# A fused retention and phase-mixing kernel: the first third of its written order laid out anew

## The chip, the cores and the metric

The kernel runs on one core of a Trainium2 chip, as one program. The metric is device time in microseconds, the median of several executions. The core has a matrix engine (TensorE, PE in the profile; its weight loads are listed apart as PEld), a vector engine (DVE), an activation engine (ACT), a general engine (POOL) and a queue engine for transfers (SP). Each runs its own list of instructions in order, and an instruction that depends on another engine's waits for its semaphore. ACT, POOL and SP also issue DMA transfers.

## The reference

Inputs are q, k, v of shape (4, 8, 768, 64) and four weights, all float32.

```python
gamma = 1.0 - 2.0 ** (-5.0 - np.arange(H))
for t in range(S):
    state = gamma * state + outer(k[:, :, t], v[:, :, t])
    y[:, :, t] = q[:, :, t] @ state / np.sqrt(D)
x = y.transpose(0, 2, 1, 3).reshape(B, S, H * D)
theta = x @ w_theta
yr = einsum('ts,bsd->btd', w_tok_r, x * cos(theta))
yi = einsum('ts,bsd->btd', w_tok_i, x * sin(theta))
u = x + yr + yi
out = u + maximum(u @ w_ch, 0)
```

A recurrence with a decay per head comes first, then a mixing over tokens with phases, then a layer over channels. The output is (4, 768, 512), float32.

## The kernel before, in words

The recurrence is computed in chunks: 24 units, each 256 tokens of one batch for four of the eight heads (unit n: batch n // 6, chunk n % 6 // 2, half of the heads n % 2). The mixing works on 24 tiles C of 128 tokens by 512 channels, six to a batch; the units 2i and 2i + 1 make the tiles 2i and 2i + 1.

Nothing is scheduled by a program: the string `ORDER` (lines 22 to 86) names 929 steps, and the loop at line 616 records them one after another. Each engine executes its share of them in that order. A step is `name.numbers.engine`; the last letter says who does it: p POOL, v DVE, a ACT, s SP (for loads and stores a and s are the queue that issues the transfer). The steps that matter here:

- Lk, Lq, Lv (lines 163 to 170, issue at 157): load k, q, v of a unit, 256 KB each. The built program gives the transfers of SP and ACT eight semaphores in turn, so each one waits until the one eight before it has landed, whichever of the two queues it is on.
- Pth, Pw.r.g, Pch (173, 182, 176): theta's weight (wth), the token weights in three row groups each (r = 0 real, 1 imaginary; g of 1, 2 and 3 blocks of 128 rows, 192, 384 and 576 KB in bfloat16), the channel weight (wch). POOL issues them, and they become bfloat16 on the way.
- const8, const9 (line 233): the decay factors qx, eight exponentials on ACT, const8 for the first 256 tokens, const9 for the rest. const7 brings in the sine table.
- ck, cq, cqs, cv (137/139, 302, 308): cast or scale k, q, v to bfloat16 (kqb, vb).
- Tk, Tq (316) transpose k and q on PE into one bank kq_ps; E copies it out as kqT.
- A (346): scores; m (355): their mask, on DVE, into at; Y (423): scores times v; I (411): state times q; ST (373): the unit's new state. S0, S1 (391, 395) carry the state on, SB copies it as bfloat16 for I.
- XB, XA (139/137, 441): the unit's result becomes xT, half of a tile. Tx (455) transposes the tile back, Ex copies it as x_sb.
- Hh.C (469): theta, four matmuls into a bank of the tag acc; CN.C.w (476): its cosine and sine, on ACT, into cs (two buffers); z.C (483): x times both.
- Tw.r.t (491) transposes a block of rows of a token weight, Ew copies it to wtr or wti.
- M.t.s (509): the two matmuls of the token mixing for output tile t and source tile s; M.t.* needs Tw and Ew of row block t % 6. u, Tu or Du, Eu, O, f, SO: the sum with x, its transpose, the channel layer, the result, its store.
- Z (278): filler, two matmuls of zeros each.

PSUM has two banks for the tag acc (Z, Hh, M, O) and two for tr (kq_ps, x_ps, w_ps, u_ps); a step that writes a bank waits until the last reader of what stood there is done. So Hh.C waits until CN has read the theta that had the bank, and Tk, Tx, Tw wait for E, Ex, Ew.

```python
def load_unit(name, src, n, e):
    t = io.tile([P, HU, 2, D], FT, ..., bufs=9 if name == "vf" else 16)
    queues[e].dma_start(out=..., in_=...)

def CN(C, w):
    st["cs", C] = work.tile([P, 2, dm], BF, name="cs", bufs=2)
    nc.scalar.activation(st["cs", C][:, w, :], st["th_ps", C], AF.Sin, ...)
```

Of the kernel before, what the change touches and what calls it, by code (L numbers as in the profile page):

```python
# [45 lines left out]
Lv.11.s XB.9.1.a XB.9.0.a f.2 M.4.0 O.1 M.4.1 cqs.14.p m.10 S0.10.v f.1 cq.11.a ck.12.v M.4.4 M.4.2
Tu.3 Eu.3.a Dx.9 SB.10.0.a cqs.12.p u.4 Hh.9 Tq.11 ck.11.v Tu.4 z.6.v Eu.4.v ck.15.v M.5.0 M.5.4
Tk.11 E.11.a SB.10.1.p cv.11.p M.5.2 M.5.3 I.10 M.5.5 M.5.1 Lq.13.a A.11 Y.10 ck.14.v ST.11 CN.9.1
CN.9.0 SO.0.a Hh.8 u.5 S0.11.v z.9.v XB.10.0.v m.11 Dk.12 Tx.8 Tq.14 O.4 Lv.13.a SB.11.0.a Lq.15.s
Lk.13.s CN.8.1 Lk.18.a XB.10.1.a CN.8.0 SB.11.1.p cv.12.p Lq.16.s I.11 Tk.14 Ex.8.v A.12 Y.11 ST.12  # L50
f.4 Lv.15.s O.3 z.8.p E.14.a XA.11.0 XA.11.1 Hh.10 S0.12.a f.3 SB.12.0.v Tx.10 Tu.5 CN.10.1 Dx.11
Ex.10.v cq.13.p Lk.16.s Lv.17.s Hh.11 SO.2.s CN.10.0 m.12 S1.12 z.10.v Tk.15 M.6.1 M.6.2 M.6.0 M.6.3
CN.11.0 CN.11.1 M.7.3 SB.12.1.a Lk.17.a ck.13.a M.7.4 M.7.0 M.6.4 Dk.13 M.7.1 z.11.v M.6.5 SO.3.s
A.14 M.7.2 Eu.5.v I.12 Lv.14.s u.6 cqs.15.v M.7.5 M.9.3 Tq.15 ck.17.a E.15.a m.14 SO.4.a Lq.17.s
Lq.18.s Lk.21.s ck.16.a M.9.0 M.9.5 M.9.1 M.9.4 Lq.19.a M.9.2 Du.6 cv.13.v u.7 M.8.0 u.9 Y.12
cv.14.p ST.13 A.13 O.5 XB.12.1.a XB.12.0.a M.8.1 S0.13.a S1.13 M.8.4 M.8.3 SB.13.0.a SB.13.1.p
cq.16.p m.13 I.13 ck.18.a Y.13 ST.14 A.15 f.5 cq.17.v Lv.18.a M.8.5 M.8.2 XA.13.0 XA.13.1 S0.14.v
SB.14.0.p Lv.16.s Hh.13 S1.14 u.8 Tx.12 M.10.1 cv.15.p cv.17.p SB.14.1.p M.10.0 M.10.4 cqs.18.v
M.10.5 CN.13.0 CN.13.1 Hh.12 CN.12.1 I.14 m.15 Y.14 CN.12.0 ST.15 S0.15.v XB.14.1.a SB.15.0.a M.10.3
cv.16.v Dk.16 Dk.17 Du.7 Dx.13 M.10.2 Dk.18 O.6 SB.15.1.p XB.14.0.v S1.15 I.15 Y.15 ST.16 SO.5.a  # L60
cv.18.p f.6 S0.16.v A.16 M.11.4 SB.16.1.p M.11.1 Lq.21.a Ex.12.a z.12.p SB.16.0.a Lk.19.s Lk.20.s
XB.15.0.a u.10 z.13.p XB.15.1.a m.16 O.7 Du.10 I.16 Y.16 ST.17 f.7 A.17 Tu.8 Hh.15 CN.15.1 CN.15.0
# [9 lines left out]
cv.21.v u.14 A.21 ST.21 CN.19.0 CN.19.1 S0.21.v M.15.3 M.15.5 S1.21 m.21 XA.20.1 Hh.18 CN.18.1  # L72
CN.18.0 Dx.18 Dk.22 ck.23.a M.15.4 M.15.2 SB.21.0.p M.15.1 M.15.0 SB.21.1.v Lv.23.s Du.12 Dx.19
XA.20.0 O.9 f.9 I.21 Y.21 A.22 ST.22 M.16.1 cqs.23.p u.15 m.22 S0.22.v z.18.p z.19.p M.16.5
SB.22.0.p M.16.4 O.12 M.16.0 SO.8.a M.16.2 M.16.3 SB.22.1.p XB.21.0.a XB.21.1.a SO.11.s Du.14
cv.23.p Dk.23 f.12 Du.13 Dx.20 Dx.21 Hh.21 u.16 I.22 A.23 Y.22 ST.23 CN.21.0 CN.21.1 Hh.20 CN.20.1
# [570 lines left out]
```

## Time and profile before

| | |
|---|---|
| time, median of 3 runs | 165.22 us (165.19 to 165.68) |
| span of the profiled execution, from its first to its last instruction | 163.6 us |
| TensorE busy | 155.2 us, 95% |
| DVE, ACT, POOL busy | 114.0, 78.9, 74.3 us |
| moved by DMA | 34.93 MB, 214 GB/s over the span |

The profile is of one execution of its own, and its span leaves out what lies ahead of the first and behind the last instruction; the times of the runs include that. The difference to the median is 1.6 us. Lines such as L476 are lines of the kernel; copies made through the helper `copy` all stand at L137 (ACT) or L139 (DVE and POOL), so the tile names tell them apart. In a group, "out<-in" are tiles. The time in brackets is how long the engine stood idle just before, and whose work ended that.

### The profile page before, as it was taken

To read this page: it belongs to the slowest core of one execution; us is meant where nothing else is said; L and a number is where in the kernel's file an instruction comes from. 1 tells how busy PE (TensorE), PEld (TensorE's weight loads), DVE (VectorE), ACT (ScalarE), POOL (GpSimd) and SP (SyncE) were. 2 spreads that over 40 slices of the span, in tenths; PEclk is the share of its full clock that TensorE was granted. 3 is DMA by queue.
4 is the path that set the end of the run, shared out by engine and by line. 5 is a ranking of instruction groups with operands and counts; after the bars stand their busy time and mean duration, and the time that the engine had idled before them with its cause. 6 is when DMAs were issued, how large, how long until landed. Compare 5 with 4: busy or idle time off the path is not lost.

```text
span 163.6 us, 4928 instructions
## 1 busy us (share of the span) xinstructions
PE 155.2 (95%) x2034; PEld 87.2 (53%) x2034; DVE 114.0 (70%) x215; ACT 78.9 (48%) x140; POOL 74.3 (45%) x107
## 2 busy tenths in 40 slices
...
GB/s 115 297 290 255 268 283 236 275 220 286 220 162 232 223 291 139 338 203 270 324 263 198 134 268 221 242 193 298 125 245 136 103 92 227 160 64 128 129 164 224
DMA packets 69062, 34.93 MB, mean 214 GB/s; under 512 B 26416, under 2 KB 66096, under 8 KB 69040
## 3 DMA queue, kind: packets, MB, share of 16 engines
...
q0 software_dynamic: 2688, 3.41, 12.1%
...
q14 instruction: 6, 0.05, 0.1%
...
## 4 chain that ended last, share of the span: by engine, by line
PE 76%; DMA 8%; ACT 5%; POOL 3%; issue 2%; SPq 2%; DVE 1%; POOLq 0%; ACTq 0%
PE y_ps L509 36%; PE o_ps L536 11%; PE th_ps L469 10%; DMA kqf<-in_k_dram 8%; PE r_ps L423 3%; ACT qx L233 3%; PE w_ps L491 3%; PE at_ps L346 3%; PE r_ps L411 2%; PE kq_ps L316 2%; SPq L157 2%; PE y_ps L561 2%; ACT cs L476 1%; PE x_ps L455 1%; PE r_ps L373 1%
## 5 line engine op out<-in xcount | busy, mean ns | idle before, releaser
L509 PE MATMUL y_ps<-z,wtr 128*128 128x512 bf16 x138 | 52.4, 380 | 0.0
L509 PE MATMUL y_ps<-z,wti 128*128 128x512 bf16 x138 | 52.3, 379 | 0.0
L483 POOL TENSOR_TENSOR z<-cs,x_sb 128x1024 bf16<-128x1024 bf16 x12 | 25.5, 2136 | 17.9 <-ACT cs L476 10.0
L355 DVE TENSOR_TENSOR at<-at_ps,mask 128x1024 bf16<-128x1024 f32 x24 | 29.2, 1216 | 0.2
L469 PE MATMUL th_ps<-wth,xT 128*128 128x512 bf16 x96 | 24.5, 379 | 0.5 <-ACT cs L476 0.4
L516 DVE TENSOR_TENSOR u<-y_ps,x_sb 128x512 bf16<-128x512 f32 x23 | 15.8, 688 | 12.7 <-PE y_ps L509 12.6
L542 DVE SCALAR_TENSOR_TENSOR ot<-o_ps,u 128x512 f32<-128x512 f32 x22 | 15.1, 688 | 12.5 <-PE o_ps L536 12.4
L308 POOL TENSOR_TENSOR vb<-vf,vsc 128x512 bf16<-128x512 f32 x15 | 15.6, 1041 | 17.3 <-DMA vf<-in_v_dram 16.9
L476 ACT ACTIVATE cs<-th_ps,zerob 128x512 bf16<-128x512 f32 x24 | 16.4, 685 | 13.3 <-PE th_ps L469 8.8
L536 PE MATMUL o_ps<-wch,uT 128*128 128x512 bf16 x88 | 22.6, 379 | 0.0
L476 ACT ACTIVATE cs<-th_ps,halfpi 128x512 bf16<-128x512 f32 x24 | 16.3, 686 | 11.5 <-issue 5.4
L509 PEld LDWEIGHTS <-wtr 128*128 128x128 bf16 x138 | 13.5, 98 | 12.7
L509 PEld LDWEIGHTS <-wti 128*128 128x128 bf16 x138 | 13.5, 98 | 12.0 <-issue 0.2
L139 POOL CAST sbd<-s 64x256 bf16<-64x256 f32 (+1 forms) x21 | 10.1, 481 | 20.8 <-DVE s L391 17.7
L137 ACT COPY kqT<-kq_ps 128x1024 bf16<-128x1024 bf16 x12 | 12.1, 1012 | 11.9 <-PE kq_ps L316 11.9
L469 PEld LDWEIGHTS <-xT 128*128 128x128 bf16 x96 | 8.8, 98 | 8.7 <-issue 0.5
L137 ACT CAST kqb<-kqf 128x512 bf16<-128x512 f32 x16 | 9.6, 620 | 6.9 <-DMA kqf<-in_k_dram 6.3
L536 PEld LDWEIGHTS <-uT 128*128 128x128 bf16 x88 | 8.1, 98 | 8.3
L278 PE MATMUL zz<-zero 128*128 128x512 bf16 x30 | 10.3, 476 | 1.9 <-DVE zero L192 1.9
L423 PE MATMUL r_ps<-at,vb 64*64 64x128 bf16 x384 | 9.9, 221 | 1.6 <-DVE at L355 1.6
L316 PE MATMUL kq_ps<-ident,kqb 128*128 128x128 bf16 x120 | 11.2, 220 | 0.3 <-POOL kqb L302 0.3
L139 POOL CAST kqb<-kqf 128x512 bf16<-128x512 f32 x12 | 7.2, 612 | 8.5 <-DMA kqf<-in_k_dram 8.4
...
## 6 DMA issues: line engine op xcount, KB each, us to landing
...
```

The source lines that it names most:

```text
L137: nc.scalar.copy(dst, src)
L139: engines[e].tensor_copy(dst, src)
L308: engines[e].tensor_mul(in_blocks(vb), by_token(raw["vf", n]), _bcast_last(K["vsc"][:, i, :, h * HU:(h + 1) * HU], D))
L355: nc.vector.tensor_mul(at.rearrange("p g j a t -> p (g j) (a t)"), st["at_ps", n].rearrange("p g j a t -> p (g j) (a t)"), _bcast_mid(K["m ...
L423: nc.tensor.matmul(st["R", n + 1][c][g * D:(g + 1) * D, j * P:(j + 1) * P], st["vb", n][rows, lo:lo + D], st["at", n][rows, g, j, a, :], s ...
L469: nc.tensor.matmul(th_ps, st["xT", C][:, j, :], K["wth"][:, j, :], start=(j == 0), stop=(j == 3))
L476: nc.scalar.activation(st["cs", C][:, w, :], st["th_ps", C], AF.Sin, bias=K["zerob" if w else "halfpi"], scale=1.0)
L483: engines[e].tensor_mul(st["z", b][:, c], st["cs", C], _bcast_mid(x_of(C), 2))
L509: nc.tensor.matmul(st["y", t], K["wT"][r][:, s0, t0 * P:(t0 + 1) * P], st["z", b][:, s0, r, :], start=(done == 0 and r == 0), stop=(done = ...
L516: nc.vector.tensor_add(st["u", t], st["y", t], st["x", b][:, t0, :])
L536: nc.tensor.matmul(o_ps, st["uT", t][:, j, :], K["wch"][:, j, :], start=(j == 0), stop=(j == nD - 1))
L542: nc.vector.scalar_tensor_tensor(st["ot", t], st["o", t], 0.0, st["u", t], ALU.max, ALU.add)
```

## The change

`ORDER` is rewritten from its start up to the step M.3.4 (328 of its 929 steps); from M.3.4 on it is unchanged. The steps are the same ones. 47 of them are done by another engine, 12 loads are issued on the other queue, and most stand at another place. Nothing else in the code differs, except that the string is two lines shorter, so every line number behind it is lower by 2.

What moves, by kind:

- Casts and scalings: ck.2, ck.5 from ACT to POOL, cqs.2 from DVE to POOL, cqs.1 and cv.2 from POOL to DVE, cv.3 from DVE to POOL, ck.4 and cq.4 from POOL to ACT, cq.5 from ACT to DVE, and some of units 7 to 10.
- State copies: most SB up to unit 8 change engine; S0.1 goes from DVE to ACT.
- E.3 and E.6 go from ACT to DVE, Ew.1.0 and Ew.0.1 from DVE to ACT, z.2 from DVE to POOL.
- Exponentials: const8 stands behind ck.1 and the loads Lk.4 and Lq.4 instead of ahead of them.
- Theta: Pth stands behind cv.1 on POOL (ck.0, SB.0.1, cv.1, Pth), no longer behind cv.2 as well. On ACT CN.0 comes ahead of XB.3 and CN.1.0, and ck.6 and cq.6 stand on both sides of CN.1.1 instead of ck.6, cq.6 ahead of both halves of CN.1; CN.4 comes after Ew.1.0.
- Weight rows: Pw.0.1 and Pw.1.1 stand around z.0; Pw.1.2 moves behind z.2, cq.8, z.4 and ck.7, with Pch and Pw.0.2 behind it.
- Loads: Lq.1 and Lk.1 go out on ACT ahead of the exponentials; Lk.6 moves ahead of Lq.6, which goes to ACT's queue with Lv.6, Lv.7 and Lk.8; Lk.9 and Lv.8 move ahead on SP.

```diff
 ORDER = """
-const2 Lv.0.s const1 const6.v Z.29 Z.2 const5 Z.38 Lk.0.a const3 Z.35 Z.8 Lq.0.s Lv.1.s Z.28 constA
-const4 Lq.1.a const9 Lk.1.s Z.39 const8 ck.0.p Tk.0 ck.1.a cqs.0.v cv.0.v Tq.0 E.0.v Lq.4.a ST.0
-Lk.4.a cqs.1.p Tq.1 Lq.2.s S0.0.v SB.0.1.v A.0 Lk.2.s SB.0.0.p cv.1.p Lv.2.s S1.0 Z.15 I.0 Z.27 m.0
-Tk.1 E.1.a cqs.2.v Z.34 cv.2.p Y.0 ST.1 XB.0.1.a S0.1.v S1.1 SB.1.0.a Pth Lq.3.s Z.18 XB.0.0.v Tq.2
-A.1 SB.1.1.a ck.2.a I.1 m.1 Y.1 ST.2 Tk.2 const7 Z.23 XB.1.0.v Lk.3.s E.2.v XB.1.1.v A.2 ck.3.p
-S0.2.v m.2 S1.2 SB.2.1.a Z.11 cqs.3.p Tq.3 Lv.3.s Tx.0 Tk.3 Z.3 ck.4.p Lv.4.s Lk.5.s Lq.5.s Lv.5.s
-Lq.6.s Lk.6.s Lv.6.s Lq.7.s E.3.a SB.2.0.v I.2 Y.2 XB.2.1.a Ex.0.a cv.3.v cq.4.p Tk.4 Lq.8.s A.3
-ST.3 Lk.7.s S0.3.v SB.3.0.a S1.3 Lv.7.s Lk.8.s Tx.1 Tq.4 SB.3.1.p cv.4.p m.3 Pw.1.0 XB.2.0.a Ex.1.a
-I.3 Lv.8.s E.4.a ck.5.a cq.5.a Y.3 Pw.0.0 ST.4 Hh.0 S0.4.v XB.3.0.v XB.3.1.v cv.5.v CN.0.1 A.4
-CN.0.0 Tq.5 Hh.1 Tk.5 SB.4.0.p SB.4.1.a Pw.0.1 Hh.2 m.4 E.5.v I.4 Y.4 ST.5 ck.6.a Tk.6 Tx.2 cq.6.a
-CN.1.1 CN.1.0 XA.4.1 A.5 XA.4.0 m.5 Lq.9.s Ex.2.v S0.5.v z.0.p Tq.6 E.6.a CN.2.0 cv.6.p Hh.3
-SB.5.0.v Tx.3 Tw.1.0 z.1.v SB.5.1.a Ew.1.0.v Ex.3.a CN.2.1 A.6 I.5 Y.5 ST.6 XA.5.0 z.2.v Tw.0.0
-CN.3.0 Tx.4 CN.3.1 Ew.0.0.v S0.6.v XA.5.1 Ex.4.v Hh.4 CN.4.0 CN.4.1 Tw.0.1 M.0.1 Pw.1.1 z.3.v M.0.0
-Tw.0.2 Pw.1.2 Ew.0.2.a SB.6.1.a Hh.5 z.4.p SB.6.0.p Lk.9.a M.0.3 ck.7.p cqs.7.p M.0.2 CN.5.1 CN.5.0
-cq.8.v m.6 Ew.0.1.v Tw.1.1 Tw.1.2 Ew.1.1.v Lv.9.s M.0.4 M.1.0 Tx.5 Ew.1.2.v M.1.1 S1.6 Tk.7 M.1.4
-Pch Ex.5.v z.5.v cv.7.v Tq.8 Tq.7 M.1.2 E.7.a M.0.5 I.6 Y.6 ST.7 A.7 ck.8.a u.0 S0.7.v m.7 XA.6.1
-SB.7.1.a M.1.5 M.1.3 XA.6.0 Tw.1.3 M.2.5 Pw.0.2 M.2.3 u.1 S1.7 Tk.8 M.2.1 M.2.0 SB.7.0.v Ew.1.3.a
-Tu.0 I.7 cv.8.v E.8.a Lk.10.s ck.10.p cv.9.p Y.7 ST.8 A.8 cqs.9.v ck.9.v M.2.4 Du.1 Eu.0.a XB.7.1.a
-XB.7.0.v S0.8.v SB.8.0.v M.2.2 Tx.6 Tq.9 Tk.9 Lv.10.a cv.10.p Lq.10.s S1.8 u.2 m.8 O.0 E.9.a
-SB.8.1.a Hh.6 Tw.1.4 I.8 Y.8 A.9 CN.6.0 Du.2 Lq.14.s CN.6.1 Ex.6.v f.0 ST.9 Tw.0.3 Hh.7 Ew.1.4.v
-Ew.0.3.a S0.9.v Tw.0.4 M.3.0 Tw.1.5 CN.7.0 CN.7.1 M.3.2 Dx.7 M.3.1 M.3.5 M.3.3 Lv.12.s Lk.12.s
-Ew.1.5.v XA.8.1 Ew.0.4.v Lq.12.s M.3.4 u.3 S1.9 Tw.0.5 Tk.10 M.4.5 cqs.10.p XA.8.0 m.9 M.4.3 Tq.10
+Lv.0.s Lq.1.a const2 Lk.0.a const1 Lk.1.a Z.29 const6.v const5 const3 cv.0.v constA Lq.0.s Z.2 const4
+ck.0.p Z.38 const9 Lv.1.a Z.35 ck.1.a Z.8 Lk.4.a Lq.4.a Z.28 const8 Z.39 cqs.0.v cqs.1.v Z.11 Lq.2.s
+ST.0 Z.34 Tk.0 S0.0.v SB.0.0.a Tq.0 E.0.v Tq.1 SB.0.1.p Lk.2.s Lv.2.s cv.1.p Tk.1 S1.0 Lv.3.s A.0 Pth
+m.0 I.0 Lk.3.s ck.2.p Z.3 cqs.2.p Z.15 Y.0 cv.2.v E.1.a A.1 ST.1 S0.1.a S1.1 Tq.2 SB.1.1.a XB.0.0.a
+ck.3.p XB.0.1.a SB.1.0.a Tk.2 I.1 m.1 E.2.v ck.4.a Y.1 Lq.3.s ST.2 A.2 XB.1.1.a Lv.4.s Z.23 Tk.4 cq.4.a
+S0.2.v SB.2.1.v XB.1.0.v S1.2 Lv.5.s Tk.3 cqs.3.p Tq.3 SB.2.0.a m.2 Z.18 const7 Lk.5.s I.2 cv.3.p Y.2
+ST.3 XB.2.0.a E.3.v cv.4.p Lq.6.a A.3 Tx.0 Lq.5.s S0.3.v S1.3 Ex.0.a Pw.1.0 Tq.4 SB.3.0.v Lv.6.a Pw.0.0
+E.4.a Hh.0 SB.3.1.v ck.5.p CN.0.0 XB.2.1.v Tx.1 I.3 m.3 cv.5.v CN.0.1 Lk.6.s Y.3 ST.4 Hh.1 Pw.0.1
+XB.3.1.a A.4 Ex.1.v Tx.3 S0.4.v SB.4.1.v z.0.p XB.3.0.a CN.1.0 cq.5.v Tq.5 SB.4.0.a Tk.5 Hh.2 I.4 ck.6.a
+CN.1.1 m.4 Y.4 E.5.v cq.6.a z.1.v ST.5 A.5 Z.27 S0.5.v Lk.8.a Ex.3.a XA.4.1 Pw.1.1 SB.5.1.p XA.4.0 Tx.2
+SB.5.0.a Tk.6 Tq.6 CN.2.0 m.5 Ex.2.a Hh.3 I.5 E.6.v Tw.1.0 Lv.7.a Y.5 CN.2.1 cv.6.p ST.6 CN.3.0 A.6
+Tw.0.0 XA.5.0 Ew.1.0.a z.2.p Lq.8.s XA.5.1 Hh.4 Ew.0.0.v CN.3.1 S0.6.v Tx.4 M.0.0 CN.4.1 z.3.v SB.6.0.v
+S1.6 Ex.4.v Tw.0.1 Lq.7.s M.0.1 M.0.2 SB.6.1.p Tw.0.2 m.6 CN.4.0 Ew.0.1.a Ew.0.2.a cq.8.p M.0.3 Hh.5
+z.4.p I.6 Tw.1.1 Lq.9.a Tx.5 cqs.7.v Y.6 M.0.4 Ew.1.1.v Ex.5.v Lk.7.s CN.5.0 CN.5.1 ck.7.p Tq.7 z.5.v
+Tw.1.2 Tk.7 Ew.1.2.v M.1.1 M.1.4 M.0.5 cv.7.v M.1.5 Tq.8 M.1.3 ck.8.a ST.7 Pw.1.2 Lk.9.s ck.9.p u.0
+E.7.a A.7 Lv.8.s M.1.2 S0.7.v Tu.0 Eu.0.v M.1.0 Pch Lv.9.s M.2.4 M.2.1 XA.6.1 Tk.8 SB.7.0.p M.2.2 XA.6.0
+S1.7 SB.7.1.p E.8.a M.2.5 m.7 M.2.0 Pw.0.2 u.1 I.7 Tw.1.4 cv.8.p Tw.1.3 Ew.1.4.a Y.7 ST.8 S0.8.v
+XB.7.0.v A.8 SB.8.1.a M.2.3 Tk.9 XB.7.1.a cqs.9.p Tq.9 SB.8.0.p Ew.1.3.a u.2 m.8 Hh.6 E.9.a Lv.10.a O.0
+S1.8 Tw.1.5 Tx.6 Du.2 cv.9.p I.8 Lq.10.s A.9 Y.8 Lk.10.a Ex.6.a f.0 ST.9 Tw.0.3 Hh.7 Ew.1.5.v Lk.12.a
+CN.6.0 CN.6.1 Du.1 Lq.14.a CN.7.0 cv.10.p Tw.0.4 Dx.7 Ew.0.3.v CN.7.1 XA.8.1 M.3.0 S0.9.v M.3.3 ck.10.v
+Ew.0.4.v Lv.12.a M.3.5 M.3.1 M.3.2 Lq.12.s M.3.4 u.3 S1.9 Tw.0.5 Tk.10 M.4.5 cqs.10.p XA.8.0 m.9 M.4.3
...
```

75 lines of the change are left out of this document (37 added, 38 removed).

## The prediction, on record ahead of the result

> **What bounds it now.** First the page's busy line, then a table of TensorE's busy time by stage (columns after the window: its length; busy time with instruction count of PE, PEld, DVE, ACT, POOL; granted clock; DMA share; GB/s).
>
> ```profile
> span 163.6 us, 4928 instructions
> PE 155.2 (95%) x2034; PEld 87.2 (53%) x2034; DVE 114.0 (70%) x215; ACT 78.9 (48%) x140; POOL 74.3 (45%) x107
> ...
> 7.34:28.62 21.28, 17.98 (x387) 11.62 (x386) 16.62 (x33) 16.45 (x31) 15.13 (x19) 1.00 1.19 267
> 28.62:53.42 24.80, 24.79 (x382) 15.84 (x381) 20.40 (x44) 17.15 (x28) 9.36 (x11) 1.00 1.24 230
> 53.42:140.00 86.58, 86.44 (x1139) 46.85 (x1138) 63.85 (x114) 38.77 (x72) 43.72 (x45) 1.00 1.05 214
> ```
>
> TensorE is the bound, at full clock. M.3.4, the last point before which the orders differ, starts at 53.42. From 28.62 to there PE lacks 0.01 us of being full, and 0.14 us in the 86.58 us behind it; before 28.62 it lacks 3.30 us, and more hides under the modelled tails of its matmuls. The change can gain only by filling PE before 28.62, and lose only by opening holes up to 53.42. Who made the holes is in the chain of waits, read in that window (start, length, what):
>
> ```profile
> 9.32 6.61 DMA kqf<-in_k_dram
> ...
> 19.31 5.96 DMA kqf<-in_k_dram
> ...
> 25.37 1.14 ACT kqb L137 x2
> 26.51 1.17 ACT cs L476 x2
> ...
> 27.72 1.02 PE th_ps L469 x4
> ```
>
> Lk.4 lands at 15.93, Lk.6 at 25.27; ACT stands at ck.6 until then, so CN.1's sines end only at 27.67, and Hh.3, which needs the PSUM bank they read, starts at 27.72. The same bank chain (the sine of CN.n frees the bank for the theta two further on) paces PE up to Hh.5. The timelines of PE, DVE and ACT (start, length, instruction, in brackets the idle time before):
>
> ```profile
> 1.92 5.58 PE L278 MATMUL zz<-zero 128*128 128x512 bf16 x14 [1.92 <-DVE zero L192]
> 21.75 1.04 PE L469 MATMUL th_ps<-wth,xT 128*128 128x512 bf16 x4
> 27.72 1.02 PE L469 MATMUL th_ps<-wth,xT 128*128 128x512 bf16 x4 [0.39 <-ACT cs L476]
> 33.69 1.03 PE L469 MATMUL th_ps<-wth,xT 128*128 128x512 bf16 x4
> 34.55 0.38 PE L509 MATMUL y_ps<-z,wtr 128*128 128x512 bf16 x1
> 49.38 0.51 PE L491 MATMUL w_ps<-ident,row 128*128 128x128 bf16 x6
> ```
> ```profile
> 9.38 1.22 DVE L355 TENSOR_TENSOR at<-at_ps,mask 128x1024 bf16<-128x1024 f32 x1
> 12.59 1.23 DVE L355 TENSOR_TENSOR at<-at_ps,mask 128x1024 bf16<-128x1024 f32 x1
> 16.03 1.23 DVE L355 TENSOR_TENSOR at<-at_ps,mask 128x1024 bf16<-128x1024 f32 x1
> 20.01 1.22 DVE L355 TENSOR_TENSOR at<-at_ps,mask 128x1024 bf16<-128x1024 f32 x1
> ```
> ```profile
> 3.95 4.90 ACT L233 ACTIVATE qx<-pos,lscale,lgp 128x512 f32<-128x512 f32 x8 [0.43 <-POOL lgp L228]
> 26.41 0.68 ACT L476 ACTIVATE cs<-th_ps,zerob 128x512 bf16<-128x512 f32 x1
> ...
> 30.23 0.69 ACT L476 ACTIVATE cs<-th_ps,zerob 128x512 bf16<-128x512 f32 x1
> ```
>
> Hh.0 starts at 21.75, Hh.5 at 33.69, Tw.0.3 at 49.38. m.0 to m.3, the masks that release each unit's Y, stand at 9.38, 12.59, 16.03, 20.01. CN.2 ends at 30.92. Sines follow each other every 0.58 us (two in 1.17, in the chain), four theta matmuls take 0.86 (33.69 to 34.55), so 0.215 each. Small steps go by their rows in the same timelines: state copies and sums 0.29, SB 0.28 to 0.40, xT copies 0.37 to 0.42, x_sb copies 0.41 (DVE) and 0.59 (ACT), w copies 0.55 and 0.80; on PE ST 0.23, Tk, Tq and Tx 0.22, A 0.35, Y 0.25, Tw 0.34.
>
> **The change, part by part.** No operation is added or removed: 328 tokens ahead of M.3.4 are the same set in both, 47 of them computing on another engine and 12 loads on another queue; the 601 behind are identical. Unit prices, the operation by engine over 7 to 54 us (last columns: busy, mean ns):
>
> ```profile
> L137 ACT COPY kqT<-kq_ps 128x1024 bf16<-128x1024 bf16 x7 | 7.1, 1011 | 6.2 <-PE kq_ps L316 6.2
> L308 POOL TENSOR_TENSOR vb<-vf,vsc 128x512 bf16<-128x512 f32 x6 | 6.2, 1040 | 3.8 <-DMA vf<-in_v_dram 3.7
> L302 POOL TENSOR_TENSOR kqb<-kqf,qsc 128x512 bf16<-128x512 f32 x4 | 4.2, 1050 | 1.4 <-DMA kqf<-in_q_dram 1.4
> L137 ACT CAST kqb<-kqf 128x512 bf16<-128x512 f32 x7 | 4.1, 620 | 0.9 <-DMA kqf<-in_k_dram 0.9
> L139 POOL CAST kqb<-kqf 128x512 bf16<-128x512 f32 x5 | 3.0, 612 | 8.4 <-DMA kqf<-in_k_dram 8.4
> L139 DVE COPY kqT<-kq_ps 128x1024 bf16<-128x1024 bf16 x3 | 2.1, 684 | 0.5 <-PE kq_ps L316 0.5
> ```
>
> All 47, priced so, take about 2.6 us from DVE and 0.4 from ACT and put 4.7 on POOL, which idles 22 of the 46 us. What counts is when each is due.
>
> Loads first. One is 0.262 MB; at the 267 to 290 GB/s of this stage that is 0.9 to 1.0 us, and wth counts as three (below: 3.41 MB of q0 take 12.1% of the span, 5.8 us per MB, so 3.0 us). Before, the 14th load lands at 15.93 and Lk.6, the 20th, with wth ahead, at 25.27. In the new order SP isn't held up as it was:
>
> ```profile
> 8.85 0.43 ACTq L157 DMA_DIRECT2D kqf<-in_q_dram  x1
> ...
> 8.38 0.51 SPq L157 DMA_DIRECT2D kqf<-in_k_dram  x1
> 8.93 5.70 SPq L157 DMA_DIRECT2D vf<-in_v_dram  x2
> ...
> q0 software_dynamic: 2688, 3.41, 12.1%
> ```
>
> The first row is Lq.4, issued on ACT behind ck.1, at the end of eight exponentials; a load waits for the one eight before it, and so the second vf of SP's row (Lv.4) waited for Lq.4, until 14.26 (8.93 + 5.70, less 0.37 of its own issue). Now four of the exponentials (const8) stand behind ck.1, Lk.4 and Lq.4, which leave at about 7.3, when Lk.1 is in. Lk.6 is the 19th load, issued near 15 instead of 19.31: 15.5 + 5 x 0.9 + 3.0 = 23.0, or 24.0 if the first weight rows share with it; Lq.6, 20th, 0.9 later. Bounds: not before the bytes allow (23.0), not later than before (25.3). Landings go by order of issue: Lq.4, alone on ACT's queue, took 5.4 us, just behind SP's loads asked for ahead of it (the last, Lk.3, at 8.38). [...]
>
> Now the chain, with 0.05 to 0.1 us for each hand-over. m.0: seven filler pairs end at 7.34 as now; an eighth (0.43), ST.0, a ninth, Tk.0 and Tq.0 (0.23 each) put E.0 at 9.0 and m.0 at 10.2, 0.8 later than 9.38. m.1: behind m.0 (1.15) come Y.0, A.1, ST.1 (0.25, 0.35, 0.23), then S0.1, now ACT's, and S1.1 (0.29 each), which stands ahead of m.1 on DVE: 12.95, 0.4 later. m.2: 12.95 + 1.15, E.2 0.6, A.2 0.35, then S0, SB, XB, S1 (1.0, overlapping A.2): 15.75, 0.3 earlier. m.3: Lq.3, the 14th load, by 15.5; cqs.3 and cv.3 on POOL 1.05 each: 17.65; E.3 on DVE in 0.6 instead of ACT's 1.01; ST.3 at 17.85, and DVE's S0.3, S1.3, both SB.3, XB.2.1 (1.25): 19.45, 0.55 earlier.
>
> Theta. The POOL rows (Pth; Pw.1.1 with Pw.1.2; Pw.0.2; one z) and the DMA issues (KB, us to landing):
>
> ```profile
> 12.62 0.93 POOL L173 DMA_DIRECT2D wth<-in_moe_w_theta_dram  x1
> 24.17 2.12 POOL L483 TENSOR_TENSOR z<-cs,x_sb 128x1024 bf16<-128x1024 bf16 x1 [0.70 <-ACT cs L476]
> 27.24 1.53 POOL L182 DMA_DIRECT2D row<-in_moe_w_tok_i_dram  x2
> 38.43 0.74 POOL L182 DMA_DIRECT2D row<-in_moe_w_tok_r_dram  x1
> ```
> ```profile
> row<-in_moe_w_tok_r_dram POOLq DMA_DIRECT2D x1, 576.0 KB, 10.4
> wth<-in_moe_w_theta_dram POOLq DMA_DIRECT2D x1, 512.0 KB, 6.8
> ```
>
> Pth now follows cv.1 alone (Lv.1, sixth load, near 9): issued at 10.2, landed at 17.0, not 19.4. Hh.0 comes behind A.3, Tx.0, Tq.4: 18.9, against 21.75. Hh.1 behind m.3's end, Y.3 and ST.4: 21.1, done at 22.1. ACT: CN.1.0 to 22.75, SB.4.0 0.3, ck.6 (Lk.6 23.0 to 24.0) to 24.0, CN.1.1 to 24.5, against 27.67. Then ACT works without a stop: cq.6 0.55, Ex.3 0.5, SB.5.0 0.35, CN.2.0 0.6, Ex.2 0.5, CN.2.1 0.6: 27.6, against 30.92; CN.3.0 0.6, Ew.1.0 0.8, CN.3.1 0.6: 29.6; CN.4 waits for z.2, now POOL's (27.7 + 2.12 = 29.8), and ends at 31.0.
>
> PE: A.5, filler Z.27 (its bank is CN.1's), Tx.2, Tk.6, Tq.6 to 26.05; Hh.3 26.05 against 27.72; I.5, Tw.1.0, Y.5, ST.6, A.6, Tw.0.0 (1.75 together); Hh.4 28.7 (bank free since 27.6); Tx.4; M.0.0 29.8 (bank 29.6); M.0.1, M.0.2, M.0.3 and two Tw (2.4); Hh.5 at 32.15. Before, 33.69 with two M fewer (0.87). Lead: 1.54 + 0.87 = 2.4 us of PE work.
>
> What takes from it. Lv.7 moves to ACT's queue behind Ex.2. After Lk.6 come eight loads (Lq.6, Lv.6, Lq.8, Lq.7, Lk.7, Lk.9, Lk.8, Lv.8) and the first 1152 KB of weight rows, then it: 23.0 + 9 x 0.9 + 1.18 x 5.8 = 37.9 if all go ahead, 36 if the last two don't. cv.7 stands on DVE ahead of u.0 and S0.7, behind which wait M.2's bank and Pw.0.2; ST.7 wants it at 36.9: 0 to 1.7 us late, I take 0.6. The weight rows: 0 to 4 us, second rival; I take 0.1, since the queue is freer then. Behind 53.42 the order is as it was, and PE's 0.14 us of holes say that the others wait for it and come earlier with it; a load may not. One that POOL waits for today, in the view of waits:
>
> ```profile
> POOL vb L308 <- DMA vf<-in_v_dram: 13.2, 2, 9.2
> ```
>
> Such a load holds the lead only where its vb is wanted at once: 0 to 0.5, I take 0.2. Sum: 2.4 - 0.6 - 0.1 - 0.2 = 1.5 us. Span 163.6 - 1.5 = 162.1; with the 1.6 us between span and median (165.22) 163.7.
>
> **Rivals.** (1) The loads come no sooner than before, since the DMA engines were full anyway (267 GB/s) and bytes don't shrink. Lk.6 at 25.3: CN.1.1 ends at 26.5, all behind it 2.0 later, lead 0.4: 164.8 to 165.2. Against it: Lk.6 has one load less ahead, and wth left 2.4 earlier.
>
> (2) The weight rows come late; slower. POOL issues Pw.1.2 behind z.2 (to 29.8), SB.6.1, cq.8, z.4 (31.1 to 33.25) and ck.7: 33.85, not 28.0; Pch and Pw.0.2 follow. From 27.24 to 48.83 (38.43 + 10.4) POOL's queue moved 384 + 576 + 512 + 576 KB, 2.10 MB, 97 GB/s. At that pace the last three, 1.70 MB, are in at 51.4; Tw.0.3 can't start sooner, against 49.38; Tw.1.5 (0.34) is then already done: M.3.4 1.7 later, 166.9. It costs the lead below 120 GB/s (Tw.0.3 due at 48.1) and makes the kernel slower below 107. For it: the pace before. Against: SP and ACT loads of units 8 to 10 shared that time; now units 8 and 9 are asked for by 33, and SP then stands at Du.2 until u.2 near 44. q0's 5.8 us per MB is 172 GB/s when alone.
>
> (3) The queues share evenly. Each load then takes 1.8 us while two queues are busy: Lq.3 lands near 18, m.3 moves to 21.2, Lk.6 near 27 behind ACT's Lq.6, Lv.6 and the rows; CN.1.1 ends at 28.2, 0.5 later than before: 165.7 to 166.5. Against: the 5.4 us of Lq.4. [...]
>
> **How the numbers follow.** Forecast 0.56, rival 1 0.15, rival 2 0.21, rival 3 0.08. 0.3% (0.5 us) is about what a measurement can tell here. Faster: the forecast and 0.06 of rival 1: 0.62. Same: 0.09 of rival 1, 0.02 of rival 3: 0.11. Slower: the rest, 0.27. The forecast's own range is 162.7 (all 2.4 us kept) to 164.6. The range takes in rivals 1 and 3 and most of rival 2: 162.6 to 166.7.
>
> **What would show it.** Right: m.1 near 12.95 but m.3 near 19.5; Hh.0 near 19; ck.6 without a wait beyond 24; CN.2 done near 27.6; Hh.5 near 32; M.3.4 near 51.7. Wrong: Lk.6 landing at 25 (1), PE idle ahead of Tw.1.3, Tw.1.4 or Tw.0.3 with row as releaser (2), POOL standing at cqs.3 until 18 (3), PE idle ahead of ST.7 for over 1 us.

## The result, and the profile after

| | before | changed |
|---|---|---|
| median, first series (5 executions each) | 165.38 us | 172.65 us (169.62 to 176.41) |
| median, second series (11 and 6) | 165.56 us | 171.91 us (170.72 to 172.80) |
| span of the profiled execution | 163.6 us | 174.7 us, in the second series 170.9 us |

The change makes the kernel slower: 1.0275 times the time before (95% interval 1.0227 to 1.0323) in the first series and 1.0373 (1.0332 to 1.0415) in the second. (The ratios leave out executions more than 1.5% above the fastest of their kernel, in the first series three of the changed kernel's five; the two that count kept the full clock.) The forecast was 163.7.

The page's busy lines, and rows of the table of windows (window, its length, busy time with count of PE, PEld, DVE, ACT, POOL, granted clock, DMA share, GB/s):

```profile
span 174.7 us, 4897 instructions
...
PE 155.7 (89%) x2006; PEld 88.4 (51%) x2034; DVE 117.9 (68%) x209; ACT 77.6 (44%) x141; POOL 80.7 (46%) x112
```
```profile
24.00:28.00 4.00, 1.69 (x30) 0.76 (x24) 3.94 (x6) 1.17 (x3) 2.78 (x2) 1.00 1.17 257
28.00:32.00 4.00, 3.77 (x64) 2.52 (x66) 2.64 (x5) 2.55 (x6) 0.00 (x0) 0.57 1.15 229
...
60.00:65.00 5.00, 1.92 (x13) 1.07 (x12) 1.72 (x3) 1.71 (x3) 2.31 (x2) 0.76 1.32 200
65.00:70.00 5.00, 4.67 (x59) 2.20 (x58) 2.41 (x4) 1.17 (x3) 2.21 (x3) 0.56 1.07 208
```

PE has the same work and is busy about as long as before (155.7 against 155.2 us), but the span grew by 11.1 us. There are two holes, at 24 to 28 and at 60 to 64, and behind each the granted clock stays near half for a few us (0.57 in 28 to 32 us, 0.56 in 65 to 70). The second hole lies behind 60.1, in the part of the order that is unchanged. The timeline of PE names the engine that ended each hole (start, length, instruction, in brackets the idle time and its releaser):

```profile
20.01 1.02 PE L467 MATMUL th_ps<-wth,xT 128*128 128x512 bf16 x3
...
23.50 0.42 PE L421 MATMUL r_ps<-at,vb 64*64 64x128 bf16 x16 [0.98 <-DVE at L353]
...
23.97 1.04 PE L467 MATMUL th_ps<-wth,xT 128*128 128x512 bf16 x4
...
28.01 0.67 PE L314 MATMUL kq_ps<-ident,kqb 128*128 128x128 bf16 x8 [2.33 <-DVE kqb L137]
...
63.59 0.61 PE L409 MATMUL r_ps<-kqT,sbd 128*128 128x128 bf16 x4 [3.08 <-ACT sbd L135]
```

Hh.0 (20.01) is earlier than before (21.75), as was meant. But Y.3 waits for m.3, and Tq.5 for cq.5 on DVE. Here is what DVE and POOL did then, and all the cv that DVE does, in this kernel and in the one before (count, then min/median/max in ns):

```profile
20.35 1.38 DVE L137 CAST sbd<-s 64x256 bf16<-64x256 f32 x2
...
22.22 1.22 DVE L353 TENSOR_TENSOR at<-at_ps,mask 128x1024 bf16<-128x1024 f32 x1
23.36 3.28 DVE L306 TENSOR_TENSOR vb<-vf,vsc 128x512 bf16<-128x512 f32 x1
...
27.53 0.43 DVE L137 CAST kqb<-kqf 128x512 bf16<-128x512 f32 x1
```
```profile
20.54 1.04 POOL L306 TENSOR_TENSOR vb<-vf,vsc 128x512 bf16<-128x512 f32 x1 [2.29 <-DMA vf<-in_v_dram]
...
23.94 2.14 POOL L481 TENSOR_TENSOR z<-cs,x_sb 128x1024 bf16<-128x1024 bf16 x1
```
```profile
L306 DVE TENSOR_TENSOR vb<-vf,vsc x8: 675/682/3280, 4.9 to 126.9; 128x512 bf16<-128x512 f32 x8
```
```profile
L308 DVE TENSOR_TENSOR vb<-vf,vsc x9: 676/681/694, 6.8 to 116.1; 128x512 bf16<-128x512 f32 x9
```

cv.5, an operation of 0.68 us, took 3.28 and ended 0.56 after z.0 on POOL (26.64 against 26.08). The two casts SB.3 took 1.38 together where a free one takes 0.29; they ended 0.15 after POOL's cv.4. So DVE seems to stand until the POOL instruction beside it is over. No cv on DVE was stretched before.

The second hole, in the timeline of ACT and then in the chain of waits (start, length, what):

```profile
56.62 0.68 ACT L474 ACTIVATE cs<-th_ps,zerob 128x512 bf16<-128x512 f32 x1
62.30 0.37 ACTq L155 DMA_DIRECT2D vf<-in_v_dram  x1
62.71 0.82 ACT L135 CAST sbd<-s 64x256 bf16<-64x256 f32 x2 [5.41 <-DMA uT<-u]
```
```profile
53.70 8.57 DMA uT<-u
62.28 0.02 issue
62.30 0.37 ACTq L155
62.67 0.04 issue
62.71 0.40 ACT sbd L135
```

The transposition Du.1 lands at 62.28; at once ACT issues a load of v, Lv.12, and then makes the copies SB.9 for which PE's I.9 waits. In the built program, and by the semaphore numbers in the trace, Lv.12 is the transfer that waits for Du.1's semaphore: Du.1 landed at 62.28, Lv.12 was issued at 62.30. It is not the eighth behind Du.1 but the third (Du.1, Lq.14, Dx.7, Lv.12). A transfer does wait until the one that had its semaphore before has landed (all 126 behind the first eight did, in the trace of the changed kernel), but that need not be the one eight before it, as was said ahead of the prediction, for the eight semaphores are not dealt out strictly in turn. Of the 126 in each kernel, 59 wait for the one eight before in the changed kernel and 69 in the kernel before; the others wait for one that is 3 to 13 places ahead. By a count of eight Lv.12 would have waited for Lv.10, which POOL read at 55.13. Before, Lv.12 waited for Lk.9, and SP issued it, where a wait holds up no cast.

### The profile page after: what moved, and what is told of

Read it like the earlier page. It is cut to its first block, busy times and chain, and to the rows that moved or that the text cites. A ratio compares the mean times of both kernels' runs of the same rounds, so it can differ in the third digit from the quotient of the medians.

```text
span 174.7 us, 4897 instructions
## 1 busy us (share of the span) xinstructions
PE 155.7 (89%) x2006; PEld 88.4 (51%) x2034; DVE 117.9 (68%) x209; ACT 77.6 (44%) x141; POOL 80.7 (46%) x112
## 4 chain that ended last, share of the span: by engine, by line
PE 70%; DMA 12%; DVE 7%; issue 4%; POOL 2%; ACT 1%; SPq 1%; ACTq 1%; POOLq 0%; DVEq 0%
PE y_ps L507 31%; PE o_ps L534 11%; PE th_ps L467 9%; DMA uT<-u 5%; DMA kqf<-in_q_dram 4%; PE r_ps L421 4%; DMA kqf<-in_k_dram 3%; PE at_ps L344 3%; PE r_ps L409 3%; PE kq_ps L314 3%; DVE vb L306 2%; PE y_ps L559 2%; PE w_ps L489 2%; PE r_ps L371 1%; DVE at L353 1%
## 5 line engine op out<-in xcount | busy, mean ns | idle before, releaser
L507 PE MATMUL y_ps<-z,wti 128*128 128x512 bf16 x130 | 49.5, 381 | 1.1 <-issue 1.1
L507 PE MATMUL y_ps<-z,wtr 128*128 128x512 bf16 x132 | 50.1, 379 | 0.3
L481 POOL TENSOR_TENSOR z<-cs,x_sb 128x1024 bf16<-128x1024 bf16 x13 | 27.5, 2126 | 14.3 <-ACT cs L474 10.1
L137 POOL CAST sbd<-s 64x256 bf16<-64x256 f32 (+1 forms) x23 | 10.9, 476 | 34.0 <-DVE s L389 22.4
L306 POOL TENSOR_TENSOR vb<-vf,vsc 128x512 bf16<-128x512 f32 x16 | 16.8, 1053 | 16.2 <-DMA vf<-in_v_dram 12.5
L534 PE MATMUL o_ps<-wch,uT 128*128 128x512 bf16 x85 | 23.9, 402 | 0.3 <-issue 0.2
L409 PE MATMUL r_ps<-kqT,sbd 128*128 128x128 bf16 x80 | 9.0, 228 | 5.8 <-ACT sbd L135 4.2
L135 ACT COPY kqT<-kq_ps 128x1024 bf16<-128x1024 bf16 x10 | 10.1, 1012 | 8.6 <-PE kq_ps L314 8.6
L135 ACT CAST xT<-r_ps 128x256 bf16<-128x256 f32 x19 | 6.6, 372 | 13.6 <-PE r_ps L371 6.6
L409 PEld LDWEIGHTS <-sbd 128*128 128x128 bf16 x80 | 6.3, 102 | 11.5 <-ACT sbd L135 4.5
```

Of the source, the lines that this page charges most:

```text
L135: nc.scalar.copy(dst, src)
L306: engines[e].tensor_mul(in_blocks(vb), by_token(raw["vf", n]), _bcast_last(K["vsc"][:, i, :, h * HU:(h + 1) * HU], D))
L409: nc.tensor.matmul(r[c][:, j * P:(j + 1) * P], sbd_of(n)[:, c, j, :], st["kqT", n][:, 1, :, j, c * D:(c + 1) * D], start=(j == 0), stop=Fa ...
L481: engines[e].tensor_mul(st["z", b][:, c], st["cs", C], _bcast_mid(x_of(C), 2))
L507: nc.tensor.matmul(st["y", t], K["wT"][r][:, s0, t0 * P:(t0 + 1) * P], st["z", b][:, s0, r, :], start=(done == 0 and r == 0), stop=(done = ...
L534: nc.tensor.matmul(o_ps, st["uT", t][:, j, :], K["wch"][:, j, :], start=(j == 0), stop=(j == nD - 1))
```

## The experiments

Theories as they were held: **A**, ACT stands at Lv.12; **B**, POOL holds DVE; **D**, three copies that the change put ahead of m.3; **E** and **G**, the clock behind a hole; **F**, what is left without these. All times are medians, beside the kernel before on the same chip (165.5 to 165.7).

**e1_loads_back.**

```diff
-... Ew.1.5.v Lk.12.a CN.6.0 CN.6.1 Du.1 Lq.14.a CN.7.0 ... Dx.7 Ew.0.3.v ... Ew.0.4.v Lv.12.a M.3.5
+... Ew.1.5.v CN.6.0 CN.6.1 Du.1 Lq.14.s CN.7.0 ... Dx.7 Lv.12.s Lk.12.s Ew.0.3.v ... Ew.0.4.v M.3.5
```

> The changed kernel with three loads (Lk.12, Lq.14, Lv.12) taken off ScalarE's queue and issued by SyncE, as the kernel before does. Theory A (the second hole is ScalarE's own stream standing at the issue of Lv.12 until the transposition Du.1 has landed, 57.3 to 62.3 us, with casts of the state behind it): PE's idle stretch at 60 to 64 us goes (3.1 us), the granted clock in 65 to 70 us returns from 0.56 to 1.0 (2.2 us), ScalarE shows no idle stretch of 5 us before sbd, and the time falls by 3 to 6 us, to 167 to 170 us. Rival (the order behind the change is simply late, by loads that land late): the hole stays, casts then wait for PE or DMA, and the time stays within 1.5 us of 172.6.

169.29 us, 1.0218 (1.0170 to 1.0267). ACT has no wait of 5 us and PE none at I.9; clock 1.0. In this execution the hole ahead of Tq.5 is 1.00 us, for cv.5 took 0.68; the cast behind it, SB.4.1, took 1.56 in its stead. DVE and POOL:

```profile
23.04 0.68 DVE L306 TENSOR_TENSOR vb<-vf,vsc 128x512 bf16<-128x512 f32 x1
...
24.29 1.56 DVE L137 CAST sbd<-s 64x256 bf16<-64x256 f32 x1
```
```profile
23.34 2.36 POOL L481 TENSOR_TENSOR z<-cs,x_sb 128x1024 bf16<-128x1024 bf16 x1
```

Which of the two is held can't be read from where their rows begin. The row of cv.5 begins ahead of z.0's in the first profile too (by 0.58 us), and in e9 and x1 by the same 0.30 as here, and there it took 3.28 and 3.00 us.

**e2_z0_on_dve** and **e3_z0_after_row.**

```diff
-... S0.4.v SB.4.1.v z.0.p XB.3.0.a CN.1.0 cq.5.v Tq.5 ...
+... S0.4.v SB.4.1.v XB.3.0.a CN.1.0 cq.5.v z.0.v Tq.5 ...
```

> The changed kernel with the phase product z.0 on VectorE behind cq.5 instead of on GpSimd. Theory B (the first hole is VectorE held for the length of a GpSimd instruction that reads the same memory: cv.5 shows 3.28 us where the other eight of its kind show 0.68): cv.5 takes 0.69 us, cq.5 ends by 26.0 instead of 27.97 us, PE's idle stretch of 2.33 us before Tq.5 shrinks below 0.8 us, the clock in 28 to 32 us stays at 1.0 and the time falls by 2 to 4 us. Rival B1 (VectorE has too much to do there): taking on z.0, 0.68 us more, it ends later and the hole grows. Rival B2 (the loads for cq.5 land late): cv.5 is short but cq.5 waits for its load, hole of 2 us or more as before.

```diff
-... SB.4.1.v z.0.p XB.3.0.a ... XA.4.1 Pw.1.1 SB.5.1.p ...
+... SB.4.1.v XB.3.0.a ... XA.4.1 Pw.1.1 z.0.p SB.5.1.p ...
```

> The changed kernel with two GpSimd steps exchanged: the issue of weight rows Pw.1.1 (0.77 us) ahead of the product z.0. No work changes engines. Theory B (held by the instruction that began first): cv.5 begins before z.0 and takes 0.69 us; the stretch moves to the next VectorE cast from SBUF to SBUF that begins inside z.0 (SB.4.1 or cq.5), which then shows more than 1 us instead of 0.29 or 0.42, and ends with z.0, near 26.8 us; the hole before Tq.5 stays between 1 and 2.3 us. Rival B2 (cv.5 waits inside itself for its data): cv.5 stays at 3 us.

e2: 170.57 us, 1.0311 (1.0283 to 1.0339); cv.5 takes 0.68, PE has no hole ahead of Tq.5, although DVE has 0.68 us more to do, so B1 and B2 fall. DVE of e2:

```profile
23.03 0.68 DVE L306 TENSOR_TENSOR vb<-vf,vsc 128x512 bf16<-128x512 f32 x1
```

e3 (170.29 us, a single execution) changed no engine's work, and the stretch moved as the theory says; the hole ahead of Tq.5 is 1.52 us. DVE and POOL of e3:

```profile
23.00 0.68 DVE L306 TENSOR_TENSOR vb<-vf,vsc 128x512 bf16<-128x512 f32 x1
...
24.24 2.08 DVE L137 CAST sbd<-s 64x256 bf16<-64x256 f32 x1
```
```profile
24.01 2.16 POOL L481 TENSOR_TENSOR z<-cs,x_sb 128x1024 bf16<-128x1024 bf16 x1
```

cv.5 was over (23.68) before z.0 began and is whole; SB.4.1 began inside z.0 and ended 0.15 after it (26.32 and 26.17). The m, S0 and copies out of PSUM that ran beside POOL's work were never stretched; only operations that take all their inputs from SBUF were. In the profiles of the kernel before and of the changed one the 48 masks m took 1.20 to 1.23 us (36 of them ran beside POOL's work), the 64 sums S0 and S1 on DVE 0.27 to 0.29, the copies xT and x_sb on DVE 0.40 to 0.43. In the rows of e3 the hold lasts to the end of POOL's instruction; who starts first they don't show, as cv.5's rows under e1 tell.

**e4_both:** the edits of e1 and e2.

> Both edits together: Lk.12, Lq.14, Lv.12 issued by SyncE, and z.0 on VectorE. Theories A and B: neither hole, clock 1.0 throughout, 163.5 to 166 us (about what was forecast, the 0.8 us each that cv.2 and SB.3.1 still lose to GpSimd left in). Rival C (the clock or the loads set the end, the holes are symptoms): 168 us or more.

167.11 us (166.66 to 167.62), 1.0083 (1.0052 to 1.0114), clock 1.0. Neither long hole is left. It missed 166 by 1.1; the next run is about that.

**e5_m3_free:** e4_both and

```diff
-ST.3 XB.2.0.a E.3.v ... Tq.4 SB.3.0.v ... Hh.0 SB.3.1.v ... CN.0.0 XB.2.1.v Tx.1 I.3 m.3
+ST.3 XB.2.0.a XB.2.1.a E.3.v ... Tq.4 SB.3.0.a SB.3.1.a ... Hh.0 ... CN.0.0 Tx.1 I.3 m.3
```

> The kernel of e4_both with the state copies SB.3.0 and SB.3.1 and the copy XB.2.1 moved from VectorE to ScalarE, so that the mask m.3 follows S0.3 on VectorE at once, as in the kernel before. Theory D (in e4_both m.3 begins at 22.03, 2.0 us later than before, because three copies that the change put on VectorE stand ahead of it, one of them held 0.94 us by GpSimd): m.3 begins by 20.6 instead of 22.03, Y.3 by 21.9 instead of 23.31, PE's idle in 20 to 24 us falls from 1.79 to under 0.9 us, and the time falls by 0.8 to 1.4 us, to about 166 us. Rival (m.4, or Lk.6, sets the pace there): Y.3 comes earlier, Hh.2 and Hh.3 do not, and the time stays within 0.3 us of 167.1.

165.96 us, 1.0020 (1.0001 to 1.0039): as expected. DVE in e4_both, then DVE and PE in e5_m3_free:

```profile
20.22 1.33 DVE L137 CAST sbd<-s 64x256 bf16<-64x256 f32 x2
...
22.03 1.22 DVE L353 TENSOR_TENSOR at<-at_ps,mask 128x1024 bf16<-128x1024 f32 x1
```
```profile
20.11 1.22 DVE L353 TENSOR_TENSOR at<-at_ps,mask 128x1024 bf16<-128x1024 f32 x1
```
```profile
21.38 0.42 PE L421 MATMUL r_ps<-at,vb 64*64 64x128 bf16 x16
```

m.3 is 1.92 earlier, and Y.3 follows it at 21.38 instead of 23.31.

**e6_cv2_pool:** e5_m3_free with `cv.2.p` for `cv.2.v`. **e11_more_order** is a second execution of it.

> The kernel of e5_m3_free with cv.2 back on GpSimd, as before. Theory B again: on VectorE cv.2 took 1.51 us (0.69 alone), held by cqs.2 on GpSimd, and m.1 stood behind it; so m.1 begins at 12.9 instead of 13.78, PE's idle of 1.1 us ahead of I.1 halves, and the time falls by 0.3 to 0.8 us more. Rival: I.1 waits for ScalarE's copies SB.1 (they are behind ck.4 and the exponentials), the idle time stays and so does the time.

> The kernel of e6_cv2_pool, a second execution with its profile: what of it repeats. Theory F (with the three stalls mended the change is worth nothing: theta 2 us earlier, units no earlier than before): Hh.0 at 19.6 against 21.75 before, Hh.3 at 27.3 against 27.72, Hh.5 at 34.0 against 33.69, I.9 and Hh.9 within 0.5 us of before, PE idle ahead of Tw.0.1 0.5 us with the weight rows as releaser. Rival (its 0.15% above before is by chance and the lead of 2 us is there in another execution): Hh.9 before 59 us.

165.83 us, 1.0015 (0.9991 to 1.0040): no difference from e5 that can be measured. The stretch of cv.2 is gone, but m.1 moved only from 13.78 to 13.63, because S1.1 stands ahead of it and waits for S0.1, which ACT ends at 13.4. The rival held. In the second run (165.60) Hh.0, Hh.5 and Hh.9 begin within 0.3 us of the first (Hh.9 at 59.85 and 59.92), so no lead hides there. In between the rows differ by 0.4 (Hh.3 27.72 against 27.29), and the wait for weight rows at Tw.0.1, expected at 0.5 us, is not in it: PE comes there 0.4 later.

**e7_lk0_first:** e6_cv2_pool with Lk.0 and Lq.1 exchanged on ACT's queue.

> The kernel of e6_cv2_pool with Lk.0 issued ahead of Lq.1 on ScalarE's queue, as before. The changed kernel issued it second, and it landed at 7.07 instead of 5.3 us, ck.0 on GpSimd ran from 7.08 and m.0 began at 10.88 instead of 9.38 us. If the order of the two loads is what is late at the start, m.0 moves to 10.0 or earlier and the time falls by 0.5 to 1.2 us more, to 164 to 165.3 us, near or below the kernel before. Rival: cqs.0, whose load Lq.0 is only the fifth asked for, sets ST.0 and m.0 anyway, m.0 stays past 10.6 us and the time is the same.

166.13 us, 1.0021 (0.9998 to 1.0044). m.0 went from 10.72 to 10.49 only; the rival held. It shows that POOL can be held as well: ck.0 on POOL, beside cqs.0 and cqs.1 on DVE, took 1.14 us in e6 and takes 0.60 here, where it runs without them. Two of the ten executions took 169 and 170 us, which no profile caught.

**e8_fillers_in_holes:** the changed kernel with Z.40 to Z.43 ahead of Tq.5 and Z.44 to Z.49 ahead of I.9.

> The changed kernel with all its waits, and filler products on zeros in its two long holes: four pairs (1.7 us) ahead of Tq.5, six pairs (2.6 us) ahead of I.9. No work of the kernel is taken away. Theory E (part of the loss and all of the spread between executions is the clock that TensorE loses behind a hole of over 2 us): granted clock 1.0 in every execution, times within 1.5 us of each other and at the lower end of the changed kernel's (169.6 to 176.4), 169 to 170.5 us. Rival (the spread comes from elsewhere, as the order in which loads land): the times spread over 4 us or more as before, or the fillers cost their own 4 us and the median exceeds 172 us.

174.88 us, 1.0565 (1.0517 to 1.0613): tight (174.47 to 175.79), but not lower; 169 to 170.5 was expected, and the rival (over 172) held. The clock had gone to half before the first fillers (0.61 in 24 to 28 us), the fourth pair waited for the bank of a sine, and the fillers ended later than the holes. Clock and fillers can't be told apart in it.

**e9_lv12_moved:** the changed kernel with Lv.12.a moved up on the same queue, behind Lk.12.a.

> The changed kernel with one load, Lv.12, asked for earlier on the same ScalarE queue: right behind Lk.12 instead of behind Dx.7. Theory A in its narrow form (what holds ScalarE is not the queue but the count: a load waits for the transfer eight before it in the program, for Lv.12 the transposition Du.1, landed at 62.28): Lv.12 now waits for an older load and goes out at once; the transfer that falls on a transposition is now Lq.14, which waits for Du.2 (issued at 51.74, landed near 56.5), so ScalarE stands 2 to 2.5 us instead of 5.0, earlier, and I.9 comes 2.5 to 3.1 us sooner: 168.5 to 170.5 us, as in e1_loads_back. Rival (loads on ScalarE's queue cost by their number and bytes): 171.5 us or more, the hole at I.9 stays above 2 us.

ACT does as expected:

```profile
55.99 0.38 ACTq L155 DMA_DIRECT2D kqf<-in_q_dram  x1
56.47 0.69 ACT L474 ACTIVATE cs<-th_ps,halfpi 128x512 bf16<-128x512 f32 x1 [1.19 <-DMA uT<-u]
...
57.76 0.82 ACT L135 CAST sbd<-s 64x256 bf16<-64x256 f32 x2
```

Now Lq.14 waits for Du.2, ACT stands 1.19 us, and I.9 waits for nothing. So it is the transfer that a load waits for that decides, not the queue alone. The expectation named it by a count of eight; in the built program Lq.14 is the sixth behind Du.2. The time, 170.61 us, 1.0312 (1.0271 to 1.0353), is just outside the range given. The first hole is as it was (2.05 us, and clock 0.57 at 28 to 32 us in the profiled execution), and PE waits 0.23, 0.41 and 0.34 us at 66 to 71 us for casts of q, k and v; whether their loads are late because of the move wasn't tried.

**e10_hole2_filled:** e2_z0_on_dve with six pairs Z ahead of I.9.

> The kernel of e2_z0_on_dve (its second hole is left in) with six pairs of filler products ahead of I.9, 2.6 us, which the hole hides; the wait stays. What the time falls by is the clock's price of that hole alone. Theory E: granted clock 1.0 in 55 to 70 us, where e2_z0_on_dve had 0.66 in 60 to 65 (1.7 us of PE work at full speed lost), I.9 at the same time or up to 0.5 us later, and 168.5 to 169.5 us instead of 170.57. Rival (the clock lost there costs nothing because others set the pace): 170.6 us or more.

171.48 us, 1.0347 (1.0312 to 1.0383). A miss: clock 1.0 behind I.9, but in this execution it was short at 20 to 28 us (0.88, 0.69), and Du.1 landed later. Inconclusive.

**e12_rows_and_copies:** e6_cv2_pool with Tw.0.1 behind M.0.1 and M.0.2, and SB.1.0.a ahead of XB.0.0.a.

> The kernel of e6_cv2_pool with two steps set by what its own trace shows late: Tw.0.1 (which waits 0.53 us for its weight rows) behind M.0.1 and M.0.2, and the state copy SB.1.0 ahead of the two copies XB.0 on ScalarE (PE idles 1.13 us ahead of I.1 behind them). Theory F: the row wait goes (0.5 us), the 1.13 us at I.1 shrink to 0.5 or less, but Y.1 right behind I.1 waits for m.1 (end 14.85), so of that at most 0.3 us counts: 164.9 to 165.5 us, at or below before. Rival (what is gained is given back at Lv.11's cast, 0.40 us at 65 us, whose load lands when it lands): 165.5 to 166 us.

166.07 us, 1.0026 (1.0004 to 1.0047). A miss: the wait for rows went from Tw.0.1 to the next block (0.33 us at 35.0), the wait at I.1 shrank from 1.13 to 1.00, and the load of v at 65 us still costs 0.37.

**Four more, on what was still open** (how the loss is shared, and the spread): the changed kernel again, e1 and e2 again, and the changed kernel with fillers in every hole (one pair ahead of I.3, two ahead of Y.3, two ahead of Tq.5, six ahead of I.9).

> The changed kernel itself, more executions and a second profile. Theory G (its spread is the clock: each execution loses it behind one hole, both, or none): the times spread over 4 us or more, 169.5 to 176.5, and in the second profile the time of the execution follows the sum of what the granted clock was short of 1.0: its span less that sum is 168 to 171 us, as with 174.7 less about 5 in the first. Theory B adds that cv.5 may be short in one execution and long in another, as who begins first differs by tenths of a us. Rival (the spread is in the landing of loads): two profiles differ in the landing times of the same load by over 2 us, and not in the clock.

> The kernel of e1_loads_back (Lk.12, Lq.14, Lv.12 issued by SyncE), more executions beside the changed kernel on one chip. Theory A: median 168.5 to 169.5, that is 3 to 4 us below the changed kernel's median, spread under 2.5 us, as the second hole and its clock are gone and the first one's clock may still go. Rival: within 1 us of the changed kernel's median.

> The kernel of e2_z0_on_dve (z.0 on VectorE), more executions beside the changed kernel on one chip. Theory B: median 170 to 171, that is 1.5 to 2.5 us below the changed kernel's, with the first hole and its clock gone, the second hole and its clock left in. Rival: within 0.7 us of the changed kernel's median.

> The changed kernel with eleven pairs of filler products (0.43 us each) in its idle stretches: one ahead of I.3, two ahead of Y.3, two ahead of Tq.5, six ahead of I.9. Every wait stays, no work of the kernel is taken out. Theory G: granted clock 1.0 in every window, the spread falls under 1.5 us, and the median is that of the changed kernel's best executions, 169.5 to 171 us (up to 1 us of the fillers is not hidden). Rival 1 (the spread comes from elsewhere): it stays at 4 us or more. Rival 2 (the fillers are themselves in the way, as the 4 us later end of e8_fillers_in_holes may say): tight, but 173 us or more.

x1 171.91; x2 169.69, 1.0241 (1.0204 to 1.0279), 2.2 us lower; x3 171.33, 1.0270 (1.0224 to 1.0315), 0.6 lower and spread over 3.9 us; x4 173.03 (172.75 to 173.29), 1.0444 (1.0424 to 1.0465). So x2 fell short of the 3 to 4 us. By the medians x3 is where its rival has it (within 0.7); by the ratios, 1.0270 against 1.0373, it is 1.7 us lower. Theory G missed in x1: the times spread over 2.1 us, not 4 or more, and the span of its profile (170.9) less the clock lost (about 3.4) is 167.5, just under the 168 to 171 given. The profile of x1 has both stalls again, cv.5 at 3.00 us and ACT standing 5.09. x4 is the tightest of all, at clock 1.0 in every window, and no faster, which was its second rival. Why, PE shows at I.9, in x1 and in x4:

```profile
60.98 0.61 PE L409 MATMUL r_ps<-kqT,sbd 128*128 128x128 bf16 x4 [1.30 <-ACT sbd L135]
61.38 1.91 PE L534 MATMUL o_ps<-wch,uT 128*128 128x512 bf16 x4
...
64.89 1.03 PE L534 MATMUL o_ps<-wch,uT 128*128 128x512 bf16 x4
```
```profile
62.58 0.38 PE L409 MATMUL r_ps<-kqT,sbd 128*128 128x128 bf16 x4
62.80 1.03 PE L534 MATMUL o_ps<-wch,uT 128*128 128x512 bf16 x4
...
64.90 1.03 PE L534 MATMUL o_ps<-wch,uT 128*128 128x512 bf16 x4
```

The same steps from I.9 to the second O take 3.91 us in x1 and 2.32 in x4: the clock costs 1.6 us behind that hole. But the fillers let I.9 start 1.6 us later, so both are at the same place at 64.9. In x1 PE had also stood 1.28 us just ahead, for a scaling of q on POOL whose load came late. The clock is a real price, and what keeps it up cost as much here.

## Why the prediction was wrong

**Where the time went.** Over both series the changed kernel has a median of 172.6 (eleven executions), e1 169.5 and e2 170.8 (ten each). Together they give 167.1, freeing m.3 166.0, and the rest 165.8, the time before. So of 7 us the load on ACT's queue costs about 3, the hold of DVE about 2 (both with the clock lost behind them), the copies ahead of m.3 1.15 (0.8 of that is SB.3 held by cv.4), and 0.3 or less remains. Together the first two give 5.5 us, 0.6 more than the two singly, and the split between them is good to about 1 us only, since single executions spread that far.

**Step "all 47, priced so".** It failed: each was priced by a row of its own, and POOL's idle 22 us were counted as free. That POOL's work stops DVE's was nowhere in the sum, and no row shown of before has it, for there z.0 ran beside copies out of PSUM. It cost cv.5 2.6 us, SB.3 0.8 and cv.2 0.8; the first two were on the path, the third was not (e6). The profile of before does show it further on, so it could have been found: a scaling on DVE that takes 0.68 us alone took 2.10 beside two cv on POOL, and ended 0.55 after the second of them.

```profile
86.93 2.10 DVE L302 TENSOR_TENSOR kqb<-kqf,qsc 128x512 bf16<-128x512 f32 x1
```
```profile
86.44 2.04 POOL L308 TENSOR_TENSOR vb<-vf,vsc 128x512 bf16<-128x512 f32 x2
```

**Step "behind 53.42 the order is as it was".** It failed, and cost most: 0 to 0.5 us was allowed for a late load, and that load's wait was looked for on POOL. The order behind M.3.4 is indeed as it was, but Lq.14, Lk.12 and Lv.12 had been moved to ACT's queue just ahead of it. The list of the change doesn't name them, and for none of them did the prediction ask which transfer it waits for and what stands behind it on ACT. For Lv.12 the transfer is the transposition Du.1, which takes 7.7 to 8.6 us in the five profiles whose chain of waits runs through it, and SB.9 stands behind. The rule that the prediction went by, that a load waits for the one eight before it, would not have shown it: by that rule Lv.12 waits for Lv.10, long landed.

**Step "m.3: 19.45".** It failed by 2.77 (22.22). Of that 1.6 was lost ahead of m.3's own chain: S0.3 began at 19.72 where the sum has it near 18.1, since m.0, m.1 and m.2 had come 0.7, 0.8 and 1.3 late (10.88, 13.78, 17.04). The other 1.1 arose in the chain, 0.8 of it in SB.3, held by cv.4. The copies were counted, at 1.25 us, but ahead of a mask that was ready without them; the kernel before has them on ACT and POOL. With them gone m.3 begins at 20.1, so that the 0.55 us to be gained over before (20.01) was never there either: m.1 and m.2 stand at 13.63 and 16.90 in e6_cv2_pool, forecast 12.95 and 15.75.

**What was right.** The loads: cqs.3 on POOL begins at 16.07 (15.5 said, near 18 by the third rival), and in e6_cv2_pool ck.6 goes through on ACT at 24.5 without a wait, so that Lk.6 had landed by then (23 to 24 said; 25.3 by the first rival, near 27 by the third). Both rivals fall with that. That the queues share evenly, which the third assumed, no run shows: in the changed kernel Lq.3 landed at 16.0 and Lk.6 at 24.0. Hh.0 at 20.01, in e6 19.63, was said to come at 18.9. Rival 2's late rows are real but small: 0.5 to 0.6 us at Tw.0.1 in e5, e6 and e7, none in e11 and none in the changed kernel's own profile, whose holes cover them. No rival held a VectorE wait or a transfer on ACT, the range missed by 6 us.

**Where the expected gain went,** once the stalls are mended. PE in e6_cv2_pool, at Hh.3, Hh.4, Tw.0.1, Hh.5 and at a later ST:

```profile
27.29 1.03 PE L467 MATMUL th_ps<-wth,xT 128*128 128x512 bf16 x4
...
29.85 1.03 PE L467 MATMUL th_ps<-wth,xT 128*128 128x512 bf16 x4
...
32.07 0.51 PE L489 MATMUL w_ps<-ident,row 128*128 128x128 bf16 x6 [0.53 <-DMA row<-in_moe_w_tok_r_dram]
...
34.04 1.03 PE L467 MATMUL th_ps<-wth,xT 128*128 128x512 bf16 x4
...
65.40 0.32 PE L371 MATMUL r_ps<-vb,kqb 64*64 64x64 bf16 x16 [0.40 <-POOL vb L306]
```

Hh.5 at 34.04 with two M more done (0.87) is a lead of 33.69 - 34.04 + 0.87 = 0.5 us, where 2.4 was forecast: 0.7 went with Hh.1 (21.84 for 21.1), 0.5 in PE's steps up to Hh.3, which fill PE and take 4.6 us from Hh.1's end where 4.1 was counted, and 0.5 in the wait for rows; 0.2 stays open. (This is the account of e6's execution; in e11 Hh.3 begins at 27.72, as before, and the wait for rows is not there.) At Hh.9 0.3 is left, and a load of v takes 0.4 at 65. That earlier sines are worth nothing as long as the units, which feed everything behind, come no earlier, fits these rows, but it is argued: no run brought the units earlier.

No version was measurably faster than the kernel before.
